# The result's store: two DMAs of two adjacent rows, from SyncE and ScalarE, in place of one DMA of four rows

## The chip, the core and the metric

The kernel runs on one core of a Trainium2 chip. A core has five engines that run their own instruction streams and meet at semaphores: TensorE (PE, matrix products into PSUM), VectorE (DVE), ScalarE (ACT), GpSimd (POOL) and SyncE (SP, which computes nothing and here issues DMAs). DMAs are issued by an engine into a queue and carried out by 16 DMA engines; a DMA raises a semaphore when its data have landed. The metric is the device time of one execution in microseconds.

## What is computed

One token goes through an attention block with a cache of keys and values, and then through a small feed-forward block. Cut to its steps:

```python
def _A_ref(x, k_cache, v_cache, wq, wo):          # 32 query heads, 8 key heads
    q = x @ wq                                    # 512 -> 32 heads of 128
    p = _softmax(q . k_cache * Dh ** -0.5)        # 16384 cached positions
    return (p . v_cache) @ wo                     # 4096 -> 512

def _B_ref(x, w1, w2, w3, w4):
    x1 = x + hs                                   # S = 1: all shifted parts are zero, so hs = 0
    return x1 + _gelu(_layernorm(x1) @ w3) @ w4   # 512 -> 1792 -> 512

x = A_x
h = x + _A_ref(_layernorm(x), ...)
return h + _B_ref(_layernorm(h), ...)
```

The result is one row of 512 numbers in bfloat16: 1024 bytes.

## The kernel before

The kernel streams 79 MB from memory: the query weights, then keys and values of the eight key heads in four pairs (`PAIRS`), then the weights `wo`, `w3` and `w4`. For each pair VectorE transposes the keys (line 634), TensorE forms the scores (line 645), ScalarE takes exponentials (line 670) and TensorE multiplies with the values (line 685). TensorE runs this as a loop written with registers and branches (`_tensor`); all other engines run straight code.

Instructions are declared with `P.op(engine, function, r=..., w=...)`. The names in `r` and `w` are what an instruction reads and writes; from them `Program.op` finds which earlier instructions it must wait for, and `Program._run` turns that into semaphore waits ahead of the instruction. An engine issues its instructions in the order in which they are declared. A DMA has a semaphore of its own, by the name given as `dma=`, and raises it by 16 when it is done.

Behind the four pairs follows the end of the kernel, about 17 us long. `o_b` is multiplied with `wo` (line 754), summed (line 766), normalised (`row_sums`, `variances`, `inverse_root`), multiplied with `w3` (line 779), put through gelu (line 791), transposed (line 795) and multiplied with `w4` (line 805). Throughout, a row of 512 numbers is held as four quarters of 128 columns, and each quarter in 32 equal rows: partitions 0 to 31 hold the first quarter 32 times, 32 to 63 the second, and so on. Line 810 adds the last product and `xsum` into `fin`, a tile of 128 partitions and 128 columns of bfloat16, on VectorE.

The last instructions are SyncE's. It waits for `fin`, issues the store (line 813), and then waits for the store's semaphore at an empty instruction (line 815), which ends its stream. ScalarE's last instruction is `xsum` (line 799). The queue of ScalarE is used once, at the very start, where it loads the 1024 bytes of `A_x` into `x4`, four partitions of 256 bytes (line 566, through `load`, whose DMA stands on line 460). All other loads are issued by SyncE.

Of the kernel before, what the change touches and what calls it, by code (L numbers as in the profile page):

```python
# [371 lines left out]
def bass_sequential_preLN__gqa_block_cached__mixer_s_mlp__decode_kernel(  # L372
# [13 lines left out]
    with ExitStack() as ctx:  # L386
        sb = lambda name, shape, dt: ctx.enter_context(nc.sbuf_tensor(name, shape, dt))
        ps = lambda name, shape, dt: ctx.enter_context(nc.psum_tensor(name, shape, dt))
        P = Program(nc, ctx)
# [52 lines left out]
        fin = sb("fin", [128, 128], BF16)  # L442
# [42 lines left out]
        def dve(fn, r=(), w=(), bank=()):  # L485
            return P.op("DVE", fn, r, w, bank)
# [16 lines left out]
        def piece(cuts, m):  # L503
            return [lo <= m < hi for lo, hi in cuts].index(True)
# [42 lines left out]
        def inverse_root(i, n, by, beside):  # L547
# [31 lines left out]
            r=["ident_f", "x4"], w=["quarter"])  # L579
# [11 lines left out]
            r=["ident_f"], w=["row32"])  # L591
        dve(lambda e: e.tensor_reduce(maskdd[:, :], ident_f[:, :].rearrange("p (n d) -> p d n", d=4), AX.X, ALU.add),
            r=["ident_f"], w=["maskdd"])
# [3 lines left out]
        for z, src, key, of, n in ((zo, row32[:, :].rearrange("p (g n h) -> p g h n", g=2, h=REP), "zo", "row32", 4),  # L597
# [6 lines left out]
            r=["hT", (("st", 0), 0), (("st", 0), 6)] + [("v", x) for x in range(VP)], w=["xn"])  # L604
# [3 lines left out]
        for i, key in enumerate(keys):  # L608
            P.part("query", i)
            for k in range(NCH):  # L610
                pe(lambda e, k=k: e.matmul(row[:, bass.ds(P.b + P.b0, 512)], copies(xn[:, k:k + 1], 128),  # L611
                                           wq_k[:, k, bass.ds(P.c + P.c0, REP * DH)], start=(k == 0), stop=(k == NCH - 1)),
                   r=["xn"], also=[("v", x) for x in range(VP)], w=["n" if key == "mn" else key], bank=[key])
        P.part()
        for g in range(2):
            half = banks[64 * g:64 * g + 64, PAIRS * g:PAIRS * g + PAIRS, :].rearrange("p j c -> p (j c)")
            for b in range(2):
# [3 lines left out]
                    r=["n" if x == "mn" else x for x in keys[PAIRS * g:PAIRS * g + PAIRS]], w=["qcol"],  # L621
                    bank=keys[PAIRS * g:PAIRS * g + PAIRS])
        for a in range(4):
            lo, hi, at = 32 * a, 32 * a + 32, QPAD + 32 * a
# [119 lines left out]
        for n, (lo, hi) in enumerate(W4):  # L744
# [4 lines left out]
            r=["o_m"], w=["o_f"])  # L749
        dve(lambda e: e.tensor_copy(o_b[:, :], o_f[:, :]), r=["o_f", ("r", 0, 0)], w=["o_b"])  # L750

        for r_ in range(32):
            q = r_ % 4
# [3 lines left out]
               r=["o_b"] + [("r", 0, n) for n in (piece(WO, r_),) if n], w=[("O", 0)], bank=[("O", 0)],  # L757
# [4 lines left out]
        for n in range(2):  # L762
            dve(lambda e, n=n: e.tensor_copy(osum[:, 256 * n:256 * n + 256], O_ps[0][:, 256 * n:256 * n + 256]),
                r=[("O", 0)], w=[("osum", n)], bank=[("O", 0)])
        for q in range(4):
            pe(lambda e, q=q: e.matmul(h_ps[32 * q:32 * q + 32, 0:128], copies(row32[:, 0:1], 32),
                                       osum[:, q * 128:(q + 1) * 128], start=True, stop=True),
               r=[("osum", q // 2), "row32"], w=[hkey], bank=[hkey])
# [4 lines left out]
            r=["hT", (S, 0)] + [("r", 1, 0)], w=["hc"])  # L773
# [3 lines left out]
        for k in range(NCH):  # L777
            for q in range(4):
                pe(lambda e, k=k, q=q: e.matmul(s_ps[32 * q:32 * q + 32, 0, 0:FQ], hc[:, k, :],
                                                w3_sb[:, k, q * FQ:(q + 1) * FQ], start=(k == 0), stop=(k == NCH - 1)),  # L780
                   r=["hc"] + [("r", 1, n) for n in (piece(W3, k),) if n], w=[("s", 0)], bank=[("s", 0)])
# [7 lines left out]
        for n in range(2):  # L789
            lo, hi = n * NHC // 2, (n + 1) * NHC // 2  # L790
# [9 lines left out]
            r=["xs", (S, 12), (S, 13)], w=["xsum"])  # L800
        for m in range(NHC):
            if m == 4:
                pe(None)
            for o in range(4):
# [3 lines left out]
                   r=[("hcol", 2 * m // NHC)] + [("r", 1, len(W3) + n) for n in (piece(W4, m),) if n],  # L808
                   w=[hkey], bank=[hkey])
        dve(lambda e: e.tensor_tensor(fin[:, :], h_ps[:, 0:128], xsum[:, :], ALU.add), r=[hkey, "xsum"], w=["fin"],  # L810
            bank=[hkey])
        dve(None)
        P.op("SP", lambda e: e.dma_start(out[0, 0:1, :].rearrange("o (q j) -> (o q) j", q=4), fin[0:128:32, :]),
             r=["fin"], w=["out"], dma="out")
        P.op("SP", lambda e: e.nop(), r=["out"])
        P.emit()

    return nc
# [28 lines left out]
```

## Time and profile before

| what | us |
|---|---|
| median of 3 runs | 190.27 (190.14 to 190.72) |
| the profiled execution's own time | 190.87 |
| its span, first to last instruction | 189.4 |
| PE busy in the span | 131.5 (69%) |
| DVE busy | 116.6 (62%) |
| ACT busy | 14.1 (7%) |
| mean granted TensorE clock | 0.919 |
| memory read | 79.17 MB, 418 GB/s over the span |

The profile shows one execution. Its time is taken around the whole program; the span, which all views are cut from, runs from the first to the last recorded instruction, and the difference of 1.47 us lies before and behind it. Times in the views count from the span's start. The engine names with a q (SPq, ACTq) stand for an engine's own instruction sequencer: a DMA's row there is the time that the engine needed to issue it, and not the transfer. Queue q1 is SyncE's, q10 is ScalarE's, and q8 fetches instructions.

### The profile page before, as it was taken

The page shows a single profiled execution, that of the slowest core. Times are in us where ns is not written, and L with a number is a line of the kernel's source. Part 1 is how long each engine was busy: PE and PEld are TensorE (multiplying, and loading weights), DVE is VectorE, ACT ScalarE, POOL GpSimd, SP SyncE. Part 2 cuts the span into 40 slices and gives each one's busy share as a digit, 9 for nine tenths or more (in the row PEclk, how much of TensorE's full clock was granted, in tenths as well). Part 3 has the DMA queues.
Part 4 walks back from the last instruction along what each step waited for, and adds up shares of the span by engine and source line. Part 5 has one row for each costly group of instructions (what it writes and reads, how often), then busy time and mean ns, then how long its engine had stood idle before and what let it go on. Part 6 is the DMA issues. An engine that isn't in the chain of part 4 may idle for free.

```text
span 189.4 us, 2414 instructions
## 1 busy us (share of the span) xinstructions
PE 131.5 (69%) x767; PEld 51.2 (27%) x767; DVE 116.6 (62%) x136; ACT 14.1 (7%) x23; POOL 6.9 (4%) x16
## 2 busy tenths in 40 slices
PE   0109901988879419888794197988938999695982
PEld 0103400333324203333241032322413333242221
DVE  5740589689152597891525979915259996534073
ACT  3000100000040000000400000004000000410012
POOL 8100000000000000000000000000000000000022
PEclk9999985599999966999999669999996999999699
DMA  6999999999899999997999999999999999979992
GB/s 222 443 443 443 429 443 457 443 443 443 353 429 436 443 554 443 415 443 325 429 422 415 443 429 443 443 443 429 443 415 422 505 443 443 443 316 412 431 406 101
DMA packets 2753, 79.19 MB, mean 418 GB/s; under 512 B 320, under 2 KB 448, under 8 KB 576
## 3 DMA queue, kind: packets, MB, share of 16 engines
q1 hardware_dynamic: 2744, 79.17, 97.4%
q8 instruction: 1, 0.02, 0.0%
q10 hardware_dynamic: 8, 0.00, 0.0%
HBM read 79.17 MB, written 0.00 MB: 418 GB/s over the span
## 4 chain that ended last, share of the span: by engine, by line
PE 51%; DVE 35%; DMA 7%; issue 6%; ACT 0%; DVEq 0%; ACTq 0%
DVE kt L634 25%; PE banks L645 20%; PE banks L500 12%; PE banks L685 7%; DMA vb<-in_A_wq_dram 7%; PE banks L611 5%; DVE mx L659 3%; PE banks L754 2%; DVE od L704 2%; PE banks L662 1%; PE banks L707 1%; DVE od L701 1%; DVE qcol L618 1%; DVE mxd L660 1%; PE banks L805 1%
## 5 line engine op out<-in xcount | busy, mean ns | idle before, releaser
L645 PE MATMUL banks<-kt,qn 128*128 x256 | 70.0, 417 | 25.7 <-DVE kt L634 25.6
L634 DVE STREAM_TRANSPOSE kt<-kb 128x4096 int32<-128x4096 int32 (+2 forms) x25 | 70.5, 2876 | 5.2 <-PE banks L645 5.2
L645 PEld LDWEIGHTS banks<-kt,qn 128*128 x256 | 26.3, 103 | 68.8 <-issue 53.5
L500 PE MATMUL banks<-qb 128*128 128x512 bf16 x70 | 25.6, 389 | 0.6
L611 PE MATMUL banks<-vb,xn 128*128 x32 | 10.0, 491 | 6.9 <-DVE xn L602 6.9
L685 PE MATMUL banks<-vb,pt 128*32 128x512 bf16 x256 | 14.7, 379 | 0.0
L670 ACT ACTIVATE p_sb<-banks,bias 128x1024 bf16<-128x1024 f32 x4 | 4.5, 1114 | 132.8 <-DVE nmh L666 132.8
L659 DVE TENSOR_REDUCE mx<-banks 128x1 f32<-128x1024 f32 x4 | 4.9, 1225 | 14.6 <-PE banks L645 14.6
L674 DVE STREAM_TRANSPOSE pt<-p_sb 64x1024 bf16<-64x1024 bf16 x8 | 9.9, 1239 | 5.4 <-ACT p_sb L670 5.3
L500 PEld LDWEIGHTS banks<-qb 128*128 128x128 bf16 x70 | 6.7, 97 | 18.8 <-issue 18.5
L685 PEld LDWEIGHTS banks<-vb,pt 128*32 128x32 bf16 x256 | 9.3, 97 | 3.5
L618 DVE STREAM_TRANSPOSE qcol<-banks 64x1024 f32<-64x1024 f32 x4 | 4.8, 1228 | 8.2 <-PE banks L611 8.2
L701 DVE TENSOR_SCALAR od<-banks,rowc 128x128 f32<-128x128 f32 x4 | 1.4, 351 | 13.4 <-PE banks L685 13.4
L611 PEld LDWEIGHTS banks<-vb,xn 128*128 128x128 bf16 x32 | 3.9, 121 | 12.7 <-issue 10.8
L556 POOL TENSOR_SCALAR st<-st 128x1 f32<-128x1 f32 x1 | 0.2, 247 | 178.1 <-DVE st L536 178.1
L662 PE MATMUL banks<-mxd,mean 128*128 128x128 f32 x8 | 2.0, 326 | 6.6 <-DVE mxd L660 6.6
L707 PE MATMUL banks<-od,zo 128*32 128x128 f32 x8 | 1.6, 285 | 6.5 <-DVE od L704 6.5
L654 ACT ACTIVATE banks<-mean 128x1024 f32<-128x1024 f32 x4 | 4.1, 1027 | 20.3 <-DVE qcol L618 20.2
L754 PE MATMUL banks<-kb,o_b 128*32 128x512 bf16 x44 | 4.6, 550 | 1.1 <-DVE o_b L750 1.1
L694 DVE RECIPROCAL den<-banks 32x1 f32<-32x1 f32 x4 | 0.6, 156 | 7.0 <-PE banks L692 7.0
L704 DVE SCALAR_TENSOR_TENSOR od<-banks,rowc,od 128x128 f32<-128x128 f32 x12 | 4.2, 351 | 0.4
L580 PE MATMUL banks<-x,quarter 4*128 4x128 bf16 x1 | 0.3, 284 | 5.4 <-DVE quarter L578 5.4
(75 smaller groups left out, 45.7 us busy)
## 6 DMA issues: line engine op xcount, KB each, us to landing
kb<-in_A_k_cache_dram SPq DMA_DIRECT2D x8, 4096.0 KB, 25.5
vb<-in_A_wq_dram SPq DMA_DIRECT2D x1, 4096.0 KB, 12.4
kb<-in_A_wo_dram SPq DMA_DIRECT2D x1, 2560.0 KB, 24.1
kb<-in_B_w_dram SPq DMA_DIRECT2D x1, 1792.0 KB, 23.0
kb<-in_A_wo_dram SPq DMA_DIRECT2D x1, 1536.0 KB, 27.4
kb<-in_B_w_dram SPq DMA_DIRECT2D x1, 1024.0 KB, 25.1
kb<-in_B_w_dram SPq DMA_DIRECT2D x1, 640.0 KB, 26.2
kb<-in_B_w_dram SPq DMA_DIRECT2D x1, 128.0 KB, 26.1
```

What stands on the lines that cost most here:

```text
L500: P.op("PE", lambda e: e.matmul(O_ps[1][:, :], field[:, 0:128], field[:, 0:512], start=True, stop=True), r=["qb"], bank=[("O", 1)], times= ...
L611: pe(lambda e, k=k: e.matmul(row[:, bass.ds(P.b + P.b0, 512)], copies(xn[:, k:k + 1], 128), wq_k[:, k, bass.ds(P.c + P.c0, REP * DH)], sta ...
L618: dve(lambda e, g=g, b=b, half=half: e.transpose(qcol[64 * g:64 * g + 64, 2 * b:2 * b + 2, :, :].rearrange("p e m u -> p (e m u)"), half.r ...
L634: P.op("DVE", lambda e, view=view: e.transpose(view(kt), view(kb[y])), r=[("r", y, i) for i in range(RPARTS)], w=[("kt", t + i) for i in r ...
L645: pe(lambda e, n=n: e.matmul(row[:, bass.ds(P.y, 512)], qn[:, n, bass.ds(P.q, 128)], key_piece(P.k, n), start=False, stop=(n == 3), skip_g ...
L654: act(lambda e: e.activation(s_all, copies(mean4[:, 0:1], 1024), ACTF.Identity, scale=0.0), r=["mean4", "p"], w=[("s", 0), ("s", 1)], **both)
L659: dve(lambda e: e.tensor_reduce(mx[:, :], s_all, AX.X, ALU.max), r=[("s", 0), ("s", 1)], w=["mx"], **both)
L670: act(lambda e: e.activation(p_sb[:, :], s_all, ACTF.Exp, bias=bias[:, 0:1], scale=float(SCALE), accum_out=acc[:, :]), r=[("s", 0), ("s", ...
L674: dve(lambda e, g=g: e.transpose(pt[64 * g:64 * g + 64, :, :, g, :], p_sb[64 * g:64 * g + 64, :]), r=["p"], w=["pt"])
L685: pe(lambda e, l=l, ct=ct, ch=ch: e.matmul(O_ps[0][32 * ct:32 * ct + 32, :], pt[:, l, ch, :, :].rearrange("p g u -> p (g u)"), tiles[:, l ...
L704: dve(lambda e, block=block, c=c: e.scalar_tensor_tensor(od[:, :], block, rowc[:, c:c + 1], od[:, :], ALU.mult, ALU.add), r=[key, "rowc", ...
L754: pe(lambda e, r_=r_, q=q: e.matmul(O_ps[0][32 * q:32 * q + 32, :], copies(o_b[:, r_:r_ + 1], 32), wo_sb[:, r_ * D:(r_ + 1) * D], start=(r ...
```

## The change

The store of the result is split. Where SyncE stored rows 0, 32, 64 and 96 of `fin` with one DMA, it now stores rows 31 and 32, which hold the first and the second quarter, and ScalarE stores rows 95 and 96, which hold the third and the fourth. Each of the two has its own semaphore, `out0` and `out1`, and writes 512 adjacent bytes of the result. The empty instruction at the end of SyncE's stream waits for both. ScalarE gets one instruction more behind `xsum`, which waits for `fin`.

```diff
         dve(None)
-        P.op("SP", lambda e: e.dma_start(out[0, 0:1, :].rearrange("o (q j) -> (o q) j", q=4), fin[0:128:32, :]),
-             r=["fin"], w=["out"], dma="out")
-        P.op("SP", lambda e: e.nop(), r=["out"])
+
+
+        for n, by in enumerate(("SP", "ACT")):
+            lo = 64 * n + 31
+            P.op(by, lambda e, n=n, lo=lo: e.dma_start(
+                out[0, 0:1, 256 * n:256 * n + 256].rearrange("o (q j) -> (o q) j", q=2), fin[lo:lo + 2, :]),
+                r=["fin"], w=[("out", n)], dma=f"out{n}")
+        P.op("SP", lambda e: e.nop(), r=[("out", 0), ("out", 1)])
         P.emit()
```

## The prediction

> **What bounds the kernel now.** I read the page's list of engines and its chain first. For 185 of 189.4 us the core moves keys, values and weights while TensorE and VectorE work through them; the change touches none of that. So the second reading is the order of time at the end of the span:
>
> ```profile
> 186.34 1.04 PE L805 MATMUL banks<-kb,hcol 128*32 128x128 bf16 x56 [1.62 <-DVE hcol L795]
> 186.45 0.50 ACT L799 ACTIVATE xsum<-xs,st 128x128 f32<-128x128 f32 x1 [0.41 <-POOL st L788]
> 187.44 0.29 DVE L810 TENSOR_TENSOR fin<-banks,xsum 128x128 bf16<-128x128 f32 x1 [0.68 <-PE banks L805]
> 187.76 0.62 SPq L813 DMA_DIRECT2D out_dram<-fin  x1
> ```
>
> After `fin` (187.44 + 0.29 = 187.73) no compute engine has anything left. ScalarE's last work ended at 186.95, so it is free when `fin` is ready. The tail is the store alone. The wait list of SyncE gives its second half, and the list of the last line's instructions gives its end:
>
> ```profile
> SPq L813 <- DVE fin L810: 26.7, 1, 26.7
> SPq L815 <- DMA out_dram<-fin: 1.0, 1, 1.0
> ...
> L815 SPq EVENT_SEMAPHORE  x1: 17/17/17, 189.4 to 189.4; - x1
> ```
>
> So 187.76 + 0.625 of issue + 1.0 of waiting = 189.39, the end of the span. The DMA view of 188.0 to 189.4 us says what was moved in that second: eight packets on the queue of SyncE, for four rows of 256 bytes, which I read as one of data and one of completion per row.
>
> ```profile
> DMA packets 8, 0.00 MB, mean 1 GB/s; under 512 B 8, under 2 KB 8, under 8 KB 8
> ...
> q1 hardware_dynamic: 8, 0.00, 0.4%
> ```
>
> The same view cut to 188.9 to 189.1, in slices of 5 ns, has the first of them at 188.98 and the last at 189.06. The 1.0 us is thus 0.60 from the end of the issue to the first packet, 0.08 of packets, and 0.33 from the last packet to the end of the wait. **Store before: 0.62 + 0.60 + 0.08 + 0.33 = 1.63 us**, all on the path.
>
> The nearest rows for what the change adds are at the start, where ScalarE issues a DMA of four rows side by side at the moment when SyncE issues a large load:
>
> ```profile
> L460 SPq DMA_DIRECT2D kb<-in_A_k_cache_dram x8: 327/328/432, 1.2 to 122.8; - x8
> ...
> L460 ACTq DMA_DIRECT2D x<-in_A_x_dram x1: 559/559/559, 0.7 to 0.7; - x1
> L460 SPq DMA_DIRECT2D vb<-in_A_wq_dram x1: 387/387/387, 0.7 to 0.7; - x1
> ...
> L813 SPq DMA_DIRECT2D out_dram<-fin x1: 625/625/625, 187.8 to 187.8; - x1
> ```
>
> The columns are minimum, median and maximum in ns of the issue. Two things are to be seen: a DMA of 128 rows takes SyncE 328 ns to issue, and the two of four rows take 559 and 625. The number of rows is not what the issue costs. The one on ScalarE began at 0.72; its packets run from 1.67 to 1.74, and the reader on VectorE starts at 2.16 with the usual gap of about 0.03 after its releaser. That is 0.56 + 0.39 + 0.07 + 0.39 = 1.41 us for a small load on the ScalarE queue.
>
> **The change part by part.**
>
> *SyncE's store, two rows for four.* One issue replaces one. The nearest row is the store itself (same engine, direction and destination), so I take 0.62. The lower end is 0.33, the issue of a 128-row load; the upper end is +0.10, by which an issue right behind another grew (432 against 328).
>
> *ScalarE's store.* One more issue, on an engine idle since 186.95. ScalarE wakes after VectorE as fast as SyncE (`hc` at 182.91 after `st` of line 526, which ended at 182.87: 0.04). Nothing is queued behind it on ScalarE, and only SyncE's last wait asks for it. Its issue alone should take 0.56 by the row of `x`. The two issues now start together. The trace has one such meeting, at 0.72: SyncE's took 387 beside it instead of 328, so I add 0.06: 0.62. The bounds are 0.33 (as above) and 0.62 + 0.62 = 1.25, if one has to wait for the whole of the other.
>
> The Trainium skill, "Perfetto Trace Analysis", section "DMA Instruction — HWDGE (DVE, Sync)", says that one descriptor generator is shared by the issuing sequencers and locked for exclusive use, and that the wait for the lock is inside the reported duration. By that rule with the whole issue under the lock the sum would be 0.62 us more; the meeting at 0.72 does not look so, since 0.39 and 0.56 began together and the longer one ended 0.17 after the shorter.
>
> *From issue to packets.* 0.60 in this store, 0.39 for `x` on the ScalarE queue, 0.64 for the weights on SyncE (issue ended at 1.11, first packet at 1.74). I take 0.60, the same transfer's own; the lower end is 0.39. The ScalarE queue was last used at 1.74 us; but `x` was its first use, so a start after idleness is in that row already.
>
> *Packets.* Each queue now carries two rows and, by the count above, four packets: eight again in all. If the two queues run beside each other it is 0.04, if one behind the other 0.08. I take 0.08.
>
> *Last packet to end of wait.* 0.33; upper end 0.39 by `x`. The bytes and their destination are the same.
>
> *The final wait.* SyncE now waits for two semaphores, one more waiting instruction (17 ns, the median of such instructions on SyncE). Only the empty last instruction stands behind it. I take 0.02; it is nothing when the ScalarE half lands last.
>
> *Rows 31, 32, 95, 96 for 0, 32, 64, 96.* They hold the same numbers, since line 805 writes each quarter into 32 equal rows, and `fin` is whole before either store. No compute instruction changes; the earlier rows of all engines are priced at nothing because the code before line 813 is the same.
>
> **Sum.** 187.76 + 0.62 + 0.60 + 0.08 + 0.33 + 0.02 = 189.41 against 189.39: +0.02 us. The profiled execution took 190.87 for its span of 189.4, so 1.47 lie outside the span, which I leave. It was 0.60 above the median of the runs shown (190.27). On the median, rounded, the forecast is **190.3**. The number of rows is a small part of a store of this size; splitting it pays again what is fixed.
>
> The Trainium skill, "DMA: Bandwidth & Descriptors", section "Issuing engines are not separate DMA queues", has it that issuing from two engines at once saves only issue time on the sequencer. Here one issue of four rows is replaced by one of two on the longer path, so by that page there would be at most the share of 0.62 that depends on rows to win; the 328 ns of a 128-row issue agree that this share is small.
>
> **The rivals.** A tenth of a per cent is 0.19 us; 0.3% (0.57 us) is about what a measurement of this kernel can tell from no change.
>
> *The two issues queue up (slower).* Place: from 187.76, both want descriptors made. If the second starts when the first is done, the end is at 187.76 + 0.62 + 0.62 + 0.60 + 0.08 + 0.33 = 190.01, +0.62 us, **190.9**. For it: the 128-row issues that follow another on the same queue grow by 0.1, so there is something that an issue has to wait for; and SyncE's 387. Against it: the meeting at 0.72. It decides from a delay of 0.57, that is when nearly the whole issue is exclusive; a partial delay (0.1 to 0.3) gives 190.4 to 190.6 and still counts as no change.
>
> *The store gets short (faster).* If what makes the four-row issue long is the stride of 32 rows, or the number of engines its rows go to, an adjacent pair could issue in 0.33, reach its first packet 0.39 later as `x` did, and need 0.04 for packets: 0.33 + 0.39 + 0.04 + 0.33 = 1.09 against 1.63, -0.54 us, **189.7**. For it: `x`, whose rows lie side by side, took 0.22 less from issue to use than this store. Against it: `x` still took 0.56 to issue, though its rows are side by side; so the stride can be worth 0.07 at most by these two rows, and both halves would have to be short. It decides only when every part is at its lower end.
>
> *Nothing of it shows.* Adjacent rows lie in two partitions, so they may travel as two separate 256-byte rows as before; the halves are then the same store twice, side by side. This is part of my forecast: -0.1 to +0.3 us, 190.2 to 190.6.
>
> **How the numbers follow.** Forecast 0.52, wholly within 0.3%, its own range 190.0 to 190.6. Issues queued up 0.27, of which 0.26 beyond 0.3% and 0.01 within. Short store 0.21: it lies at the edge of 0.3% (189.70), so 0.14 beyond and 0.07 within. Together: faster 0.14, same 0.60, slower 0.26. The range takes in both rivals' times, 189.7 to 190.95, since either alone holds over a tenth.
>
> **What would show it.** Right: two issues of about 0.6 us starting together at 0.03 after `fin`, four packets on each of the two queues, and a last wait of about 1.0. Queued up: one issue of over 1 us, or packets of one queue half a microsecond behind the other's. Short store: issues near 0.33, or first packets 0.4 behind them. The prediction is wrong if the ScalarE queue has a cost of its own for stores, which no row here shows, or if something before `fin` moves, for which the diff gives no reason.

## The result and the profile after

The changed kernel took 189.91 us (189.69 to 190.28) where the kernel before, beside it, took 190.22. The ratio is 0.9983, with a 95% interval of 0.9975 to 0.9990: 0.32 us faster, between 0.19 and 0.48. That is less than the 0.3% which the prediction counted as no change. The time lies below the 190.0 to 190.6 of the forecast itself, and within the whole range of 189.7 to 190.95 only because that took in the rivals. The interval leaves out no effect at all, the forecast was +0.02 us, the other way, and the reason given for it was wrong.

The end of the span of the changed kernel in order of time (start, duration, engine, line, operation):

```profile
186.88 0.29 DVE L810 TENSOR_TENSOR fin<-banks,xsum 128x128 bf16<-128x128 f32 x1 [0.87 <-PE banks L805]
187.20 0.33 SPq L817 DMA_DIRECT2D out_dram<-fin  x1
187.20 0.26 ACTq L817 DMA_DIRECT2D out_dram<-fin  x1
```

Both issues start together, 0.03 us after `fin`, as forecast. They take 0.33 and 0.26 us, about half of the 0.625 of the store before. The list of the line's instructions gives the durations in ns, and SyncE's wait list the second half of the store:

```profile
L817 SPq DMA_DIRECT2D out_dram<-fin x1: 331/331/331, 187.2 to 187.2; - x1
L817 ACTq DMA_DIRECT2D out_dram<-fin x1: 256/256/256, 187.2 to 187.2; - x1
```

```profile
SPq L817 <- DVE fin L810: 27.2, 1, 27.2
...
SPq L820 <- DMA out_dram<-fin: 1.0, 1, 1.0
```

The DMA view of 187.9 to 188.1 us shows four packets on each of the two queues, eight in all as before:

```profile
DMA packets 8, 0.00 MB, mean 5 GB/s; under 512 B 8, under 2 KB 8, under 8 KB 8
...
q1 hardware_dynamic: 4, 0.00, 1.6%
q10 hardware_dynamic: 4, 0.00, 1.5%
```

Wait rows are rounded to 0.1 us, so for what follows the end of SyncE's last instruction and the starts of the first and last packet were located in narrow windows of the trace, to about 0.01 us. The stretch from the end of `fin` to the end of SyncE's last instruction is called the tail below. Before, it runs from 187.73 to 189.42, **1.69 us** (the prediction read its end 0.03 too early, from rounded rows). After, it runs from 187.17 to 188.53, **1.36 us**. The difference of 0.33 us accounts for the measured gain of 0.32.

The two profiled executions differ by 0.97 us (190.87 and 189.9), which is not the change. `fin` itself ended 0.56 us earlier in the second, behind the same instructions on TensorE and VectorE. The first of the two executions lay 0.65 above the median of its kernel, the second at its own. Only the tail is compared between traces below. Where two traces hold the same store, it repeats: 1.69 in the kernel before and 1.70 in x_again, 1.36 in the changed kernel and 1.34 in own_waits.

### The profile page after: what moved, and what is told of

It is laid out like the page before. It is cut to its first block, busy times and chain, and to the rows that moved or that the text cites. A ratio compares the mean times of both kernels' runs of the same rounds, so it can differ in the third digit from the quotient of the medians.

```text
span 188.5 us, 2414 instructions
## 1 busy us (share of the span) xinstructions
PE 130.8 (69%) x766; PEld 50.4 (27%) x767; DVE 116.6 (62%) x136; ACT 14.1 (7%) x23; POOL 6.9 (4%) x16
## 4 chain that ended last, share of the span: by engine, by line
PE 43%; DVE 28%; DMA 23%; issue 5%; ACT 0%; DVEq 0%; SPq 0%; POOLq 0%; ACTq 0%
DVE kt L634 19%; DMA vb<-in_A_v_cache_dram 16%; PE banks L645 16%; PE banks L500 9%; PE banks L685 8%; DMA vb<-in_A_wq_dram 6%; PE banks L611 5%; PE banks L754 2%; DVE mx L659 2%; DVE od L704 2%; PE banks L662 1%; DVE qcol L618 1%; PE banks L707 1%; PE banks L805 1%; DVE od L701 1%
## 5 line engine op out<-in xcount | busy, mean ns | idle before, releaser
L685 PEld LDWEIGHTS banks<-vb,pt 128*32 128x32 bf16 x256 | 8.5, 97 | 4.5 <-POOLq L482 0.3
```

What stands on the lines that cost most here:

```text
L685: pe(lambda e, l=l, ct=ct, ch=ch: e.matmul(O_ps[0][32 * ct:32 * ct + 32, :], pt[:, l, ch, :, :].rearrange("p g u -> p (g u)"), tiles[:, l ...
```

## The experiments

Each kernel below has a trace of one execution. Those for which a ratio is given were also timed repeatedly beside the kernel before; the others are judged by their trace alone. The table has the parts of the tail: the issue, the time from the start of the first issue to the first packet, from the start of the last packet to the end, and the tail itself. All are in us and from one trace each.

| kernel | rows of `fin`, DMAs | issue | start to first packet | last packet to end | tail |
|---|---|---|---|---|---|
| before | 0, 32, 64, 96 by SP | 0.625 | 1.22 | 0.36 | 1.69 |
| after | 31-32 by SP, 95-96 by ACT | 0.331, 0.256 | 0.75 | 0.54 | 1.36 |
| stride_pairs | 0, 32 by SP; 64, 96 by ACT | 0.602, 0.564 | 1.20 | 0.36 | 1.88 |
| both_on_sp | 31-32, 95-96, both by SP | 0.331 and 0.263 | 0.77 | 0.36 | 1.52 |
| single_rows | four of one row, SP and ACT in turn | 0.287 to 0.323, 0.242 to 0.270 | 0.73 | 0.56 | 1.74 |
| four_adjacent | 30-33 by SP | 0.347 | 0.78 | 0.37 | 1.24 |
| four_on_act | 0, 32, 64, 96 by ACT | 0.576 | 1.22 | 0.37 | 1.69 |
| eight_adjacent | 28-35 by SP, 128 B each | 0.367 | 0.80 | 0.35 | 1.25 |
| sixteen_adjacent | 24-39 by SP, 64 B each | 0.361 | 0.87 | 0.83 | 1.87 |
| stride_33 | 0, 33, 66, 99 by SP | 0.739 | 1.33 | 0.37 | 1.80 |
| stride_2 | 28, 30, 32, 34 by SP | 0.727 | 1.34 | 0.37 | 1.78 |
| half_sp | 31-32 by SP alone | 0.331 | 0.76 | 0.36 | 1.17 |
| own_waits | as after, two waits | 0.331, 0.257 | 0.75 | 0.52 | 1.34 |

The theories to be told apart: it is the number of rows in a DMA that counts (two for four), or it is that the rows lie side by side, or it is the second engine.

**stride_pairs: the pairs, but 32 rows apart.**

```diff
-            lo = 64 * n + 31
+            lo = 64 * n
...
-                ... fin[lo:lo + 2, :]),
+                ... fin[lo:lo + 33:32, :]),
```

> The changed kernel with rows 0 and 32, 64 and 96 (32 partitions apart) in place of 31 and 32, 95 and 96. Theory A (what counts is the number of rows per DMA, two for four): the two issues take about 0.33 us on SyncE and 0.26 on ScalarE as in the changed kernel, and the time is 0.3 us (0.17%) below the kernel before. Theory B (what counts is that the two rows lie side by side): the issues take about 0.6 us again and the gain is gone, within 0.1 us of the kernel before.

Measured: 190.44 us against 190.27, ratio 1.0008 (0.9999 to 1.0017). Its issues, from the list of the line's instructions:

```profile
L817 SPq DMA_DIRECT2D out_dram<-fin x1: 602/602/602, 187.3 to 187.3; - x1
L817 ACTq DMA_DIRECT2D out_dram<-fin x1: 564/564/564, 187.3 to 187.3; - x1
```

Two rows each, two engines, and yet 0.60 and 0.56 us. The gain is gone, and the tail is 0.19 longer than before. Theory A falls, theory B holds. Another thing is to be seen in its DMA view of 188.5 to 189.2: one burst of packets in the second slice, another about 0.27 us behind it. The first is SyncE's and the second ScalarE's. So two strided stores that start together do follow each other in part; the packets of two adjacent ones did not (all eight of the changed kernel lie within 0.04 us).

```profile
GB/s 0 29 0 0 0 0 0 0 0 0 0 0 0 0 0 0 15 15 0 0 0 0 0 0 0 0 0 0 0 0 0 0 0 0 0 0 0 0 0 0
```

**four_adjacent: one DMA of four rows side by side.**

```diff
-        ... fin[0:128:32, :]),
+        ... fin[30:34, :]),
```

> One DMA by SyncE of the four rows 30 to 33, side by side; the output then holds the first quarter twice and the second twice, and no third or fourth. Theory A (number of rows): the issue takes 0.6 us as in the kernel before. Theory B (rows side by side): about 0.33.

```profile
L815 SPq DMA_DIRECT2D out_dram<-fin x1: 347/347/347, 187.2 to 187.2; - x1
```

0.35 us for four rows by SyncE alone, against 0.625 for four rows 32 apart: theory B again. Its tail of 1.24 is even shorter than that of the changed kernel. What it stores is not the result: the third and the fourth quarter are left out.

**stride_33 and stride_2: is it the step of 32, or any step?**

```diff
-        ... fin[0:128:32, :]),
+        ... fin[0:100:33, :]),      # stride_33
+        ... fin[28:36:2, :]),       # stride_2
```

> The kernel before with rows 0, 33, 66 and 99 in place of 0, 32, 64 and 96: one DMA by SyncE, a step of 33 rows. If every step other than one row is slow, the issue takes 0.62 us and the time is the kernel before's within 0.1 us. If the slow case is the step of 32 rows alone, the issue takes 0.35 us, as for four adjacent rows, and the time falls by 0.4 us, below the changed kernel.

> One DMA by SyncE of rows 28, 30, 32 and 34; the output then holds the first and the second quarter twice. If any step other than one row is slow: an issue of 0.6 us and 0.6 us more to the first packet. If only far steps are: 0.35 and 0.43, as for rows 30 to 33.

```profile
L815 SPq DMA_DIRECT2D out_dram<-fin x1: 739/739/739, 187.0 to 187.0; - x1
```

```profile
L815 SPq DMA_DIRECT2D out_dram<-fin x1: 727/727/727, 187.3 to 187.3; - x1
```

The first line is from stride_33, the second from stride_2. Both are slow, a little slower than the step of 32; stride_33 took 190.32 us against 190.33 (ratio 1.0002, 0.9994 to 1.0011). Of the steps tried (1, 2, 32, 33) only the step of one row is quick. Nor is it where the rows lie: stride_2 and eight_adjacent both begin at row 28 and run past row 32, with 0.727 and 0.367 us of issue. The price is paid twice: about 0.3 to 0.4 us in the issue, and about 0.17 us from the end of the issue to the first packet (0.60 before and in stride_33, 0.43 in four_adjacent).

**eight_adjacent and sixteen_adjacent: does the number of rows count at all?**

```diff
-        ... q=4), fin[0:128:32, :]),
+        ... q=8), fin[28:36, 0:64]),        # eight_adjacent
+        ... q=16), fin[24:40, 0:32]),       # sixteen_adjacent
```

> One DMA by SyncE of rows 28 to 35, 64 columns each; the output is then not the result but pieces of its first two quarters. If each row of a small DMA costs about 0.15 us of issue (0.33 for two, 0.62 for four), the issue takes about 1.2 us. If DMAs of fewer than 16 rows pay one fixed extra and two rows are the exception, about 0.6.

> One DMA by SyncE of rows 24 to 39, 32 columns each; the output is then not the result but pieces of its first two quarters. If each row costs 0.15 us of issue at every count, about 2.4 us; against that stands that 128 rows take 0.33. If 16 rows, one for each of the 16 DMA engines, are the quick case that 128 rows are, about 0.33.

```profile
L815 SPq DMA_DIRECT2D out_dram<-fin x1: 367/367/367, 187.0 to 187.0; - x1
```

```profile
L815 SPq DMA_DIRECT2D out_dram<-fin x1: 361/361/361, 187.3 to 187.3; - x1
```

The first line is from eight_adjacent: 0.367 us, shorter than either of the two values expected. The second is from sixteen_adjacent: 0.361 us, near the 0.33 of its second case; but that sixteen rows are a special case falls with eight rows being as quick. For adjacent rows SyncE's issue is 0.33 to 0.37 from two rows to sixteen. With sixteen rows of 64 bytes the tail was long again, but at another place: 0.83 us from the last packet to the end, instead of 0.36. In that trace fifteen of the sixteen increments of the store's semaphore had come by 188.61 us, and the last came alone at 189.07. With one trace it is not shown that the size of the rows did this.

**both_on_sp: without the second engine.**

```diff
-        for n, by in enumerate(("SP", "ACT")):
+        for n, by in enumerate(("SP", "SP")):
```

> The two DMAs of the changed kernel, rows 31 and 32 and rows 95 and 96, but both issued by SyncE. Theory A1 (the second engine is needed because issues on one engine follow each other): 0.33 + about 0.4 us of issues, the end moves to the kernel before or up to 0.1 us behind it. Theory A2 (two short DMAs are cheaper than one of four rows wherever they are issued): part of the 0.3 us stays, 0.1 us or more below the kernel before.

```profile
L817 SPq DMA_DIRECT2D out_dram<-fin x2: 263/297/331, 187.3 to 187.6; - x2
```

Measured: 189.99 us against 190.27, ratio 0.9986 (0.9977 to 0.9995). Theory A2: a part of the gain is there with SyncE alone. By the tails it is half, 0.17 of 0.33 us. The remaining 0.16 is less than the intervals of the two times can tell apart.

**four_on_act: the old store from ScalarE.**

```diff
-        P.op("SP", lambda e: e.dma_start(..., fin[0:128:32, :]),
+        P.op("ACT", lambda e: e.dma_start(..., fin[0:128:32, :]),
```

> The store of the kernel before, one DMA of rows 0, 32, 64 and 96, issued by ScalarE in place of SyncE. If the number of rows sets the price, the issue takes 0.56 us, as ScalarE's load of four rows at the start did, and the time is at most 0.1 us below the kernel before. If ScalarE is simply the quicker issuer of stores, about 0.26 to 0.33 and 0.3 us faster.

```profile
L815 ACTq DMA_DIRECT2D out_dram<-fin x1: 576/576/576, 187.3 to 187.3; - x1
```

Measured: 190.21 us against 190.19, ratio 1.0001 (0.9992 to 1.0010), issue 0.576. ScalarE issues a little quicker than SyncE in every pair of rows here (0.256 and 0.331, 0.564 and 0.602), but it isn't what the gain comes from.

**single_rows: a DMA for each row.**

```diff
+        for n, by in enumerate(("SP", "ACT", "SP", "ACT")):
+            P.op(by, lambda e, n=n: e.dma_start(out[0, 0:1, 128 * n:128 * n + 128], fin[32 * n:32 * n + 1, :]),
+                 r=["fin"], w=[("out", n)], dma=f"out{n}")
```

> Four DMAs of one row each (0, 32, 64, 96), in turn by SyncE, ScalarE, SyncE, ScalarE. If the issue goes by the number of rows (0.62 for four, 0.33 for two), one row takes about 0.18 and two of them in a row on one engine about 0.36 to 0.45: between 0.1 us slower and 0.05 faster than the changed kernel. If there is a fixed price of about 0.3 per issue whatever the rows, two in a row take 0.6 and the gain is gone.

```profile
L816 SPq DMA_DIRECT2D out_dram<-fin x2: 287/305/323, 187.2 to 187.6; - x2
L816 ACTq DMA_DIRECT2D out_dram<-fin x2: 242/256/270, 187.2 to 187.5; - x2
```

Measured: 190.29 us against 190.27, ratio 1.0001 (0.9992 to 1.0010). A single row costs 0.24 to 0.32 us of issue, nearly what two or sixteen adjacent ones cost: the fixed price, as the second case expected. Two in a row on each engine give the gain back: the tail is 1.74. Of this, 0.07 goes to the end of SyncE's stream, where four semaphores take two waiting instructions.

**x_again: why did ScalarE's load of four adjacent rows take 0.56?** The forecast had leaned on that row.

```diff
+        load("x50", x5[0][:, :], A_x[...], "x50", "ACT")        # right behind the load of x4
...
+            if j == 1:
+                load("x51", x5[1][:, :], A_x[...], "x51", "ACT")
...
-        P.op("SP", lambda e: e.nop(), r=["out"])
+        P.op("SP", lambda e: e.nop(), r=["out", "x50", "x51"])
```

> The kernel before with two more loads of the same 1024 bytes by ScalarE into other tiles: one right behind the first, one in the middle of the kernel. The first load's issue takes 0.56 us though its four rows lie side by side. If that is a price of a small load from memory, the two more take 0.5 us or more each. If it is the price of the first issue, or of SyncE issuing at the same moment, the one in the middle takes 0.25 to 0.35 us, and the one right behind the first up to 0.1 more.

```profile
L461 ACTq DMA_DIRECT2D x<-in_A_x_dram x3: 255/260/553, 0.7 to 53.6; - x3
...
L461 SPq DMA_DIRECT2D vb<-in_A_wq_dram x1: 387/387/387, 0.7 to 0.7; - x1
```

Minimum, median and maximum of the three loads: 0.255, 0.260 and 0.553 us. Only the first is slow, the one that is the first issue of its engine and meets SyncE's. The same load costs 0.26 both right behind it and at 53.6. The two peculiarities were not separated by a run of their own, but the timeline of 1.3 to 1.6 us has the second load beside another of SyncE's issues:

```profile
1.17 0.41 SPq L461 DMA_DIRECT2D kb<-in_A_k_cache_dram  x1
1.31 0.26 ACTq L461 DMA_DIRECT2D x<-in_A_x_dram  x1
```

It lies wholly within SyncE's issue, and still takes 0.26. The stores of the changed kernel met as well, at 0.26. Both speak for the first issue as the cause, and against the meeting.

**half_sp and own_waits: what the second queue costs.**

```diff
-        for n, by in enumerate(("SP", "ACT")):                                 # half_sp
+        for n, by in enumerate(("SP",)):
...
-        P.op("SP", lambda e: e.nop(), r=[("out", 0), ("out", 1)])
+        P.op("SP", lambda e: e.nop(), r=[("out", 0)])
```

```diff
-        P.op("SP", lambda e: e.nop(), r=[("out", 0), ("out", 1)])              # own_waits
+        P.op("ACT", lambda e: e.nop(), r=[("out", 1)])
+        P.op("SP", lambda e: e.nop(), r=[("out", 0)])
```

> The changed kernel without ScalarE's DMA: the second half of the result is not stored. From the end of fin to the end of SyncE's wait the changed kernel took 1.36 us, one DMA of four adjacent rows 1.24. If the two queues disturb each other, SyncE's pair alone takes 1.2 to 1.25. If they don't, 1.33 to 1.38.

> The changed kernel with each engine waiting for its own DMA at its end: SyncE for out0, ScalarE for out1. In the changed kernel 0.54 us pass from the last packet to the end of SyncE's wait for both, against 0.33 to 0.36 in the kernels with one queue. If the double wait costs that, the time falls by 0.1 to 0.2 us below the changed kernel (0.4 to 0.5 us below the kernel before). If the completions themselves come late, it is the changed kernel's: 0.3 us below the kernel before.

SyncE's wait list in half_sp:

```profile
SPq L820 <- DMA out_dram<-fin: 0.8, 1, 0.8
```

0.8 us instead of the 1.0 of the changed kernel, with the same issue of 331 ns: the tail is 1.17, a little below the 1.2 to 1.25 expected if the queues disturb each other, and the last packet is 0.36 from the end instead of 0.54. With the other queue running, SyncE's store ends 0.18 later. It isn't the double wait: own_waits took 190.05 us against 190.29, ratio 0.9980 (0.9972 to 0.9989), which the interval can't tell from the changed kernel's 0.9983 (the quotient of its two medians, 0.9987, lies in the interval too), and SyncE's own store, waited for alone, still ended 0.52 behind the last packet. Its two waits show more:

```profile
L820 ACTq EVENT_SEMAPHORE  x1: 17/17/17, 188.5 to 188.5; - x1
```

```profile
L821 SPq EVENT_SEMAPHORE  x1: 17/17/17, 188.7 to 188.7; - x1
```

ScalarE's wait ended 0.18 before SyncE's, although the packets of the two stores were only 0.02 apart, ScalarE's first. ScalarE's store thus ended 0.37 behind its own last packet, as a store alone does. Only the store whose packets came second is late. In single_rows the semaphores of the four stores were raised at 188.29, 188.48, 188.66 and 188.84 us: 0.18 apart each, though their packets were 0.10, 0.21 and 0.10 apart. In both_on_sp, whose packets are 0.35 apart, neither store is late. That looks as if the completions of such stores follow one another at least 0.18 us apart; why was not tried. No correct kernel here is measurably better than the changed one. One DMA of four adjacent rows would be 0.12 shorter in the tail (1.24 against 1.36), but the four quarters meet in adjacent rows only in pairs.

## Why the prediction was wrong, point by point

- *The tail is the store alone, and it is all on the path.* Right: a tail shorter by 0.33 us gave 0.32 us of time.
- *SyncE's store, two rows for four: 0.62.* This is the step that failed. It measured 0.331, the lower end that I had set from the 128-row loads. I had chosen the store itself as the nearest row because it shared the engine and the direction. What it did not share was the step between rows, and that set the price: 0.60 at a step of 32 with two rows, 0.35 at a step of one with four.
- *The stride can be worth 0.07 at most, because `x`, whose rows lie side by side, took 0.56.* The inference behind that choice, and wrong. One row with two peculiarities, first issue of its engine and issued beside another, was read as the price of a small adjacent DMA; the same load repeated cost 0.26. The step was worth 0.28 in the issue (0.625 against four_adjacent's 0.347).
- *ScalarE's store: 0.62.* Measured 0.256. The meeting of the two issues did not lengthen SyncE's: 331 with ScalarE's beside it, 331 without it (half_sp).
- *From issue to packets: 0.60.* Measured 0.44 from the end of SyncE's issue to its own first packet (187.53 to 187.97), near the lower end of 0.39. The very first packet, at 187.945, is ScalarE's.
- *Packets: 0.08, or 0.04 if the queues run beside each other.* 0.04 for all eight, and 0.02 for SyncE's four.
- *Last packet to end of wait: 0.33, upper end 0.39.* Measured 0.54, outside the bounds (0.36 in the trace before, read finely). Here the second queue does cost something, at the one place where I had expected nothing. It took back 0.18 of what the issue and the start had gained. Along SyncE's store, which ends last: -0.29 in the issue, -0.16 to its first packet, -0.06 in packets, +0.18 at the end, together -0.33.
- *The final wait: 0.02.* It measured 28 ns for two semaphores where the wait for one took 17, so 0.01; own_waits, without it, has a tail shorter by 0.02.
- *The rival that came nearest* was the short store, at 0.21. Its mechanism, the stride, was right for the issue and the first packet, and it was priced at -0.54; it gave -0.33, mostly because the end grew. Both halves were short, as it required. Two of the signs given for the forecast showed as well, four packets on each queue and a last wait of 1.0, the second by luck: a shorter start and a longer end made up the same 1.0. The issues alone told the two cases apart.
- *The two issues queue up.* Not with adjacent rows. With strided ones it happened in part: 0.27 us between the two queues' first packets in stride_pairs.
- *The sentence that splitting pays again what is fixed* is what single_rows and both_on_sp show, but it was not what this change turned on. The Trainium skill, "DMA: Bandwidth & Descriptors", section "Issuing engines are not separate DMA queues", says that a second issuing engine saves issue time alone. The runs agree in part: between both_on_sp and the changed kernel the second engine saves 0.31 us of issue, with the gap before it, and 0.04 to the first packet, but loses 0.19 at the end, so that 0.16 us of tail remain. The other half of the gain, 0.17, came from the shape of the DMAs alone. The shape is also what the second engine needs: with strided pairs (stride_pairs) the tail is 0.19 longer than before.

## What to carry to other kernels

A small store out of SBUF at the end of a kernel is all on the path, and its price is not its bytes or its rows: from one row to sixteen the issue cost 0.24 to 0.37 us when the rows were adjacent, and 0.56 to 0.74 when they were not, with about 0.17 us more to the first packet. Where a result lies in equal copies, choose the copies that are neighbours, and count what a second DMA costs in its own right (0.18 us at the end here). And before a duration is taken from the nearest row, list in what that row differs from the planned instruction: a first issue of an engine is a poor price for a later one.

## What was not expected of the hardware

- A step between partitions other than one (2, 32, 33 tried) adds 0.25 to 0.4 us to the issue of a store of two or four rows and about 0.17 us from there to its first packet. The longer issue shows on SyncE and on ScalarE alike.
- ScalarE's first DMA issue took 0.55 us, the same load later 0.26.
- Two adjacent-row stores on two queues begin their packets 0.02 us apart, but the second of them is done 0.18 us later than it is alone. Four single-row stores were done 0.18 us apart each.
- Sixteen rows of 64 bytes are issued as fast as four of 256, and were done 0.47 us later after their last packet (0.83 against 0.37), by one late increment out of sixteen, in one trace.
